# Longer weight runs through a permuted head layout, and a down projection that makes a row in four column tiles

## The chip, the cores and the metric

The kernel runs on one core of a Trainium2 chip. The metric is the device time of one execution in microseconds (us). Executions of the same kernel differ, so a difference of one microsecond needs several runs.

## The reference

One decoding step of one transformer block with adaptive layer norm: batch 1, width D = 640, 32 heads of 128, a cache of 16384 positions per head, a gated FFN of width F = 1728. The cut:

```
mod = silu(c) @ w_mod                       # six rows of 640: sa, ca, ga, sb, cb, gb
h = layernorm(x) * (1 + ca) + sa
for each of 32 heads: q = h @ wq ; scores = q . K / sqrt(128) ; o = softmax(scores) @ V
x = x + ga * (concat(o) @ wo)               # wo: 4096 x 640
h = layernorm(x) * (1 + cb) + sb
x = x + gb * ((silu(h @ w_gate) * (h @ w_up)) @ w_down)   # w_down: 1728 x 640
```

K and V are 32 x 2 loads of 4 MB each in bf16; everything else together is about 22 MB.

## The kernel before

Per head: VectorE multiplies the K tile by q (`mult`) and adds its halves (`fold1`); TensorE sums the rest with an identity (`fold`); VectorE finishes the scores (`red`, `max`); POOL takes the maximum over partitions (`gm`); ScalarE makes `exp`; TensorE makes P·V in four column tiles. A step called `diag` then transposes the result into a column, ScalarE scales it (`on`), and TensorE applies that head's output weights (`wo`). K and V have two buffers each. All large loads are issued in one fixed order by one queue (SP), and an issue that has to wait for a free buffer holds back all issues behind it.

The parts that matter (cuts marked ...; the numbers are positions in each engine's program):

```
# output weights: 4 heads a load, each row of wo a run of 640 * 2 = 1280 bytes
d_wo[g] = plan.dma(..., woring[:, g % 2], A_wo[g*G*128:(g+1)*G*128, :].rearrange("(g p) n -> p g n", p=128), ...)
# a V load may start only when P.V of two heads earlier is done
vdeps = [o_pvlast[h - 2]] if h >= 2 else [o_mod_a, o_mod_b]
...
# transposing step: 4 matmuls (fp32: 8 instructions) per head, then scale, then 5 output matmuls
def f_diag(e):
    for i in range(4):
        e.matmul(OT_ps[:, h:h+1], lhsT=acc_sb[:, s2, 128*i:128*(i+1)], rhs=sel[:, i:i+1], start=(i == 0), stop=(i == 3))
o_on[h] = op(ACT, vbase + 10.0, ... On[:, h:h+1] <- OT_ps[:, h:h+1] * rl[:, h:h+1])
o_wo[h] = op(PE, vbase + 10.5, ... 5 matmuls)
...
# down weights in three pieces: 1600 KB, 80 KB, 480 KB; a column of the output per 5 matmuls
NJA = FJ - 3
d_wd = [dma(wd_v[:, 0:NJA]), dma(wdr_v[0:FR]), dma(wd_v[:, NJA:FJ])]
for j in js:
    for cc in range(KC):
        e.matmul(f_ps[:, cc:cc+1], lhsT=wv[:, cc, :], rhs=gu_col[0:kw, j:j+1], ...)
# output: 128 runs of 10 bytes
d_out = plan.dma(..., out[0, 0].rearrange("(p k) -> p k", k=KC), o_col[:], ...)
```

## Time and profile before

693.03 us, median of three runs (691.93 to 693.73).

| | before |
|---|---|
| span of the profiled run | 690.0 us |
| read from HBM | 290.5 MB |
| DMA queue 1, share of 16 engines' span | 98.8% |
| DVE, PE, POOL, ACT busy | 66%, 44%, 41%, 12% |
| last weights landed (landing records) | 684.36 us |
| from there to the end | 5.65 us |

From the page of the kernel before, the slice line of the DMA engines, the packet line and two of the queues (queue: packets, MB, share):

```profile
DMA  9999999999999999999999999999999999999995
DMA packets 16398, 290.86 MB, mean 422 GB/s; under 512 B 1458, under 2 KB 7284, under 8 KB 7284
q1 hardware_dynamic: 16368, 290.48, 98.8%
q8 instruction: 20, 0.33, 0.2%
```

The engines are full from the second microsecond to the last slice: the kernel is bound by DMA. Of 16368 packets 5824 are the 1280-byte rows of output and down weights.

DMA is not busy without a break.

The packet records put the idle time of the average engine between 650 and 660 us at 0.78 us. Why, the chain of work that ended last tells (start us, us, what; these lines are not adjacent):

```profile
650.19 3.56 PE psb L436 x30
653.77 0.33 SPq L71
...
657.13 25.75 DMA kring<-in_B_w_down_dram
```

P·V of head 29 ends at 653.77 us, and at that moment SP issues the last V load, which needs that buffer. The loads queued before it run out at about the same time.

The tail, from the timeline of the kernel before (start us, us, engine, line, operation, tiles, count, [idle before it and what ended it]; the lines of LDWEIGHTS and one of DVE left out):

```profile
680.62 0.17 DVE L515 TENSOR_TENSOR gu_col<-psb,sg 128x14 bf16<-128x14 f32 x1 [2.78 <-PE psb L506]
683.02 3.37 PE L523 MATMUL psb<-gu_col,kring 128*128 128x1 bf16 x70 [2.51 <-DMA kring<-in_B_w_down_dram]
686.43 0.16 DVE L529 TENSOR_TENSOR tt<-psb,mod_col 128x5 f32<-128x5 f32 x1 [5.63 <-PE psb L523]
686.82 0.36 SPq L71 DMA_DIRECT2D out_dram<-o_col  x1
```

PE has its operand at 680.8 us and waits for the 1600 KB piece until 682.9; then all 70 matmuls still have to run.

Last, a late head (timeline of the kernel before; lines of LDWEIGHTS, DVE and POOL left out):

```profile
593.10 0.40 ACT L421 ACTIVATE P_sb<-S_sb,nb 128x128 bf16<-128x128 f32 x1
593.41 0.18 ACT L421 ACTIVATION_READ_ACCUMULATOR P_sb<-S_sb,nb 128x1 f32 x1
593.50 0.24 ACT L462 ACTIVATE On<-psb,rl 128x1 bf16<-128x1 f32 x1
593.64 0.39 ACT L385 ACTIVATE R_sb<-ident,q_r 128x128 bf16<-128x128 bf16 x1
...
593.80 0.36 PE L470 MATMUL psb<-On,woring 128*128 128x1 bf16 x5 [10.04 <-ACT On L462]
...
594.30 3.48 PE L436 MATMUL psb<-vring,P_sb 128*32 128x512 bf16 x32
```

Each ScalarE instruction starts about 0.1 us before the one ahead of it ends. From the end of the exp instruction (593.50) to P·V it is 0.80 us, and it is 0.80 to 0.81 us in each of the twelve heads whose P·V follows an exp directly rather than waiting for V (the first, the last ones and the one after the long wait for V at 527 us, which have less ahead of P·V, apart).

### The profile page before, as it was taken

What the parts mean: (1) busy time and instruction counts of PE and PEld (TensorE: products, weight loads), DVE (VectorE), ACT (ScalarE), POOL (GpSimd) and SP (SyncE); (2) the same over time, 40 slices, a digit from 0 to 9 for tenths busy, and PEclk for the clock granted to TensorE, in tenths of its full rate; (3) what the DMA queues carried; (4) which work ended last, traced back from release to release, by engine and by line L of the source; (5) the groups of instructions that cost most, each with busy time, mean ns of one, the idle gap of its engine ahead of it and who ended that gap; (6) DMA issues with size and microseconds to landing.
All of it is one profiled execution on the core that took longest, in us unless ns stands there. A gap on an engine that the chain in (4) does not pass through costs nothing.

```text
span 690.0 us, 5939 instructions
## 1 busy us (share of the span) xinstructions
PE 305.9 (44%) x2602; PEld 150.5 (22%) x2602; DVE 453.8 (66%) x151; ACT 80.1 (12%) x306; POOL 280.4 (41%) x75
## 2 busy tenths in 40 slices
PE   1503454545444334455432455444335345454464
PEld 1401122222212122222111222212112122221144
DVE  0077767676778876657787566668766676767800
ACT  0100101111111111110111111101011011111110
POOL 0006666565677554000405033304054365667700
PEclk9997666666767666666766666657666666767675
DMA  9999999999999999999999999999999999999995
GB/s 385 422 423 435 434 427 428 427 431 429 430 419 433 434 431 434 420 438 426 430 433 425 432 429 428 427 428 429 437 432 421 434 432 427 425 433 424 400 425 202
DMA packets 16398, 290.86 MB, mean 422 GB/s; under 512 B 1458, under 2 KB 7284, under 8 KB 7284
## 3 DMA queue, kind: packets, MB, share of 16 engines
q1 hardware_dynamic: 16368, 290.48, 98.8%
q8 instruction: 20, 0.33, 0.2%
q14 instruction: 6, 0.05, 0.0%
q10 hardware_dynamic: 4, 0.00, 0.0%
HBM read 290.47 MB, written 0.00 MB: 421 GB/s over the span
## 4 chain that ended last, share of the span: by engine, by line
DMA 40%; DVE 21%; PE 18%; POOL 18%; ACT 2%; issue 1%; SPq 1%
DMA kring<-in_A_k_cache_dram 36%; POOL gm L417 18%; DVE kring L397 13%; PE psb L407 9%; PE psb L436 7%; DVE f L399 6%; DMA kring<-in_B_w_down_dram 4%; DVE S_sb L411 2%; ACT P_sb L421 1%; PE psb L470 1%; DVE pm L414 1%; SPq L71 1%; PE psb L523 0%; PE psb L388 0%; ACT nb L419 0%
## 5 line engine op out<-in xcount | busy, mean ns | idle before, releaser
L397 DVE TENSOR_TENSOR kring<-kring,qbc_sb 128x16384 bf16<-128x16384 bf16 x32 | 278.0, 8687 | 30.2 <-DMA kring<-in_A_k_cache_dram 28.5
L417 POOL PARTITION_ALL_REDUCE gm<-pm x32 | 136.7, 4272 | 333.5 <-DVE pm L414 327.5
L436 PE MATMUL psb<-vring,P_sb 128*32 128x512 bf16 x992 | 108.6, 616 | 138.3 <-DMA vring<-in_A_v_cache_dram 138.3
L424 POOL PARTITION_ALL_REDUCE Ls<-rs x32 | 140.7, 4396 | 27.3 <-ACT P_sb L421 27.3
L407 PE MATMUL psb<-f,ident 128*128 128x512 bf16 x512 | 135.0, 421 | 27.9 <-DVE f L399 27.9
L399 DVE TENSOR_TENSOR f<-kring 128x8192 bf16<-128x8192 bf16 x32 | 141.6, 4425 | 1.1
L411 DVE TENSOR_REDUCE S_sb<-psb 128x128 f32<-128x512 f32 x32 | 22.1, 692 | 153.2 <-PE psb L407 153.2
L470 PE MATMUL psb<-On,woring 128*128 128x1 bf16 x160 | 11.6, 182 | 160.7 <-ACT On L462 159.7
L407 PEld LDWEIGHTS psb<-f,ident 128*128 128x128 bf16 x512 | 50.7, 104 | 120.5 <-DVE f L399 49.5
L436 PEld LDWEIGHTS psb<-vring,P_sb 128*32 128x32 bf16 x992 | 33.5, 138 | 190.8 <-DMA vring<-in_A_v_cache_dram 140.4
L470 PEld LDWEIGHTS psb<-On,woring 128*128 128x128 bf16 x160 | 8.9, 130 | 162.3 <-ACT On L462 162.3
L419 ACT ACTIVATE nb<-gm 128x1 f32<-128x1 f32 x32 | 6.5, 203 | 307.6 <-POOL gm L417 307.6
L447 PEld LDWEIGHTS psb<-sel,acc_sb 128*128 128x128 f32 x248 | 32.3, 191 | 5.8 <-ACT acc_sb L441 1.2
L441 ACT ACTIVATE acc_sb<-psb 128x512 f32<-128x512 f32 x31 | 18.5, 597 | 117.9 <-PE psb L436 117.8
L447 PE MATMUL psb<-sel,acc_sb 128*128 128x1 f32 x248 | 29.4, 240 | 0.7 <-ACT acc_sb L441 0.7
L426 ACT ACTIVATE lnl<-Ls 128x1 f32<-128x1 f32 x32 | 6.4, 201 | 115.8 <-POOL Ls L424 115.8
L388 PE MATMUL psb<-R_sb,ones_bf 128*128 128x128 bf16 x32 | 8.3, 259 | 23.6 <-ACT R_sb L385 23.6
L421 ACT ACTIVATE P_sb<-S_sb,nb 128x128 bf16<-128x128 f32 x32 | 12.8, 401 | 1.0
L385 ACT ACTIVATE R_sb<-ident,q_r 128x128 bf16<-128x128 bf16 x32 | 12.5, 389 | 0.0
L391 ACT ACTIVATE qbc_sb<-psb 128x128 bf16<-128x128 f32 x32 | 8.9, 277 | 11.2 <-PE psb L388 11.2
L414 DVE TENSOR_REDUCE pm<-S_sb 128x1 f32<-128x128 f32 x32 | 9.2, 286 | 1.1
L308 POOL PARTITION_ALL_REDUCE st<-st x2 | 0.8, 391 | 20.8 <-DVE x L488 11.2
(62 smaller groups left out, 80.3 us busy)
## 6 DMA issues: line engine op xcount, KB each, us to landing
kring<-in_A_k_cache_dram SPq DMA_DIRECT2D x32, 4096.0 KB, 25.6
vring<-in_A_v_cache_dram SPq DMA_DIRECT2D x31, 4096.0 KB, 34.4
wreg<-in_A_wq_dram SPq DMA_DIRECT2D x1, 5120.0 KB, 27.1
woring<-in_A_wo_dram SPq DMA_DIRECT2D x8, 640.0 KB, 25.5
vring<-in_w_mod_dram SPq DMA_DIRECT2D x1, 4800.0 KB, 14.3
vring<-in_A_v_cache_dram SPq DMA_DIRECT2D x4, 1024.0 KB, 9.7
wreg<-in_B_w_gate_dram SPq DMA_DIRECT2D x1, 2160.0 KB, 16.7
wreg<-in_B_w_up_dram SPq DMA_DIRECT2D x1, 2160.0 KB, 21.6
```

What stands on the lines that cost most here:

```text
L397: o_mult[h] = op(DVE, base, lambda e, kslot=kslot, qb=qb: e.tensor_tensor(out=kslot, in0=kslot, in1=qb, op=ALU.mult), deps=[d_k[h], o_qbc[ ...
L399: o_fold1[h] = op(DVE, base + 8.8, lambda e, kslot=kslot: e.tensor_tensor(out=f1[:], in0=kslot[:, :, 0:64], in1=kslot[:, :, 64:128], op=AL ...
L407: r = e.matmul(S_ps[s2][:].rearrange("p (t r) -> p t r", r=GC), lhsT=ident[:], rhs=f1[:, :, GC * m:GC * (m + 1)], start=(m == 0), stop=(m ...
L411: o_red[h] = op(DVE, base + 17.0, lambda e, s2=s2: e.tensor_reduce(out=S_sb[:, s2], in_=S_ps[s2][:].rearrange("p (t r) -> p t r", r=GC), a ...
L414: o_max[h] = op(DVE, base + 19.3, lambda e, h=h, s2=s2: e.tensor_reduce(out=pm[:, h:h + 1], in_=S_sb[:, s2], axis=AX.X, op=ALU.max), deps= ...
L417: o_gm[h] = op(POOL, base + 19.6, lambda e, h=h: e.partition_all_reduce(gm[:, h:h + 1], pm[:, h:h + 1], channels=128, reduce_op=bass.bass_ ...
L421: o_exp[h] = op(ACT, base + 20.4, lambda e, h=h, s2=s2, sp=sp: e.activation(out=P_sb[:, sp, 0:TT], in_=S_sb[:, s2], func=ACTF.Exp, scale=S ...
L424: o_L[h] = op(POOL, base + 21.0, lambda e, h=h: e.partition_all_reduce(Ls[:, h:h + 1], rs[:, h:h + 1], channels=128, reduce_op=bass.bass_i ...
L436: r = e.matmul(acc_ps[s2][q4:q4 + 32, :], lhsT=P_sb[:, sp, 4 * j:4 * j + 32], rhs=vring[:, s2, 4 * j:4 * j + 4, :].rearrange("p a d -> p ( ...
L441: o_acc[h] = op(ACT, vbase + 9.0, lambda e, s2=s2: e.activation(out=acc_sb[:, s2, :], in_=acc_ps[s2][:], func=ACTF.Copy), deps=[o_pvlast[h ...
L447: r = e.matmul(OT_ps[:, h:h + 1], lhsT=acc_sb[:, s2, 128 * i:128 * (i + 1)], rhs=sel[:, i:i + 1], start=(i == 0), stop=(i == 3))
L470: r = e.matmul(attn_ps[:, cc:cc + 1], lhsT=wv[:, cc, :], rhs=On[:, h:h + 1], start=(h == 0 and cc == 0), stop=(h == H - 1 and cc == KC - 1 ...
```

## The change

The intent has two parts. **Part 1**: for seven of the eight groups of four heads, load the output weights so that a partition gets four consecutive rows, a run of 5120 bytes. Partition p then holds rows 4p to 4p+3, so the attention output has to be laid out the same way: `diag` writes it in 32-row pieces (16 fp32 matmuls, 32 instructions per head), each head is scaled on its own 32 partitions, and the output matmuls of four heads come together. **Part 2**: the down weights come in five pieces, the last of 160 KB; the down projection makes a row (each column tile 160 wide) so that four matmuls per 128 rows run side by side; gate and residual are needed as rows too; the output goes out as four runs of 320 bytes. The buffers for P also fall from 6 to 4 (NP in the diff).

The diff, cut to its core:

```
-    NP = 6
+    NP = 4
+        o_gbrmm = op(PE, 1.2, f_gbr, ...)                       # gate row, 20 matmuls at the start
-                                   A_wo[...].rearrange("(g p) n -> p g n", p=128), ...
+                                   A_wo[...].rearrange("(g p) n -> p g n" if lastg else "(p g) n -> p g n", g=G), ...
-                    for i in range(4):
-                        r = e.matmul(OT_ps[:, h:h + 1], lhsT=acc_sb[:, s2, 128 * i:128 * (i + 1)], ...)
+                    for j in range(1 if lastg else G):
+                        for i in range(4):
+                            blk = acc_sb[:, s2, 128 * i:128 * (i + 1)]
+                            if lastg: dst = OT_ps[:, h:h + 1]
+                            else:
+                                dst = OT_ps[32 * hq:32 * hq + 32, h - hq + j:h - hq + j + 1]
+                                blk = blk.rearrange("p (m j) -> p j m", j=G)[:, j, :]
+                            r = e.matmul(dst, lhsT=blk, rhs=sel[:, i:i + 1], start=(i == 0), stop=(i == 3))
+                qs = slice(32 * hq, 32 * hq + 32)
+                on_dst, on_src, on_sc = On[qs, h - hq:h - hq + G], OT_ps[qs, h - hq:h - hq + G], rl[qs, h:h + 1]
-            o_wo[h] = op(PE, vbase + 10.5, f_wo, ...)           # 5 matmuls each head
+            elif hq == G - 1:
+                o_wo[h] = op(PE, vbase + 10.5, lambda e, h=h: f_wo(e, h + 1 - G, h + 1), ...)   # 20 every fourth
-        NJA = FJ - 3
+        wd_cut = [(0, 5), (5, 9), None, (9, FJ - 1), (FJ - 1, FJ)]
+        o_x1rmm = op(PE, TE + 0.25, f_x1r, ...)                 # x1 as a row, 20 fp32 matmuls
-                for cc in range(KC):
-                    r = e.matmul(f_ps[:, cc:cc + 1], lhsT=wv[:, cc, :], rhs=gu_col[0:kw, j:j + 1], ...)
+                for g in range(4):
+                    r = e.matmul(f_ps[32 * g:32 * g + 1, 0:RW], lhsT=gu_col[0:kw, j:j + 1], rhs=wv[:, RW * g:RW * (g + 1)], ...)
-        d_out = plan.dma(..., out[0, 0].rearrange("(p k) -> p k", k=KC), o_col[:], ...)
+        d_out = plan.dma(..., out[0, 0].rearrange("(g n) -> g n", g=4), o_row[0:128:32, :], ...)
```

More of the change, by code (lines that the diff above doesn't have):

```diff
@@ L164, in build @@
     GC = 4
+    RW = D // 4
     G = 4
-    NP = 6
+    NP = 4
     LASTP = 4
@@ L215, in build @@
         sel = sb("sel", [128, GC], F32)
-        cx_row = sb("cx_row", [1, 2, D], BF16)
+        identf = sb("identf", [128, 128], F32)
+        gb_row = sb("gb_row", [128, RW], F32)
+        x1_row = sb("x1_row", [128, RW], F32)
+        t3_row = sb("t3_row", [128, RW], F32)
+        o_row = sb("o_row", [128, RW], BF16)
+        cx_row = f1[0:1].rearrange("p t d -> p (t d)")[:, 0:2 * D].rearrange("p (v n) -> p v n", v=2)
         mod_col = sb("mod_col", [128, NMOD], F32)
@@ L238, in build @@
         gu_col = sb("gu_col", [128, FCH], BF16)
-        tt3 = sb("tt3", [128, KC], F32)
-        o_col = sb("o_col", [128, KC], BF16)
         psb = [es.enter_context(nc.psum_tensor("psb%d" % i, [128, 512], F32)) for i in range(8)]
@@ L253, in build @@
         f_ps = psb[0]
+        x1r_ps = psb[1]
+        gbr_ps = psb[3]
         acc_ps = [psb[6], psb[7]]
@@ L266, in build @@
             out=sel[:], in_=ident[:].rearrange("p (g r) -> p r g", g=4)[:, 0:GC, :], axis=AX.X, op=ALU.add), deps=[o_ident], name="sel")
+        o_idf = op(DVE, 0.12, lambda e: e.tensor_copy(out=identf[:], in_=ident[:]), deps=[o_ident], name="identf")
+        o_zgb = op(DVE, 0.01, lambda e: e.memset(gbr_ps[:, 0:RW], 0.0), name="zero_gbr")
         d_c = plan.dma(-1.0, cx_row[:, 0, :], c_in[0:1, :], "c", eng="act", name="dma_c")
@@ L301, in build, with f_gbr @@
         o_mod_b = op(PE, 1.1, lambda e: f_mod(e, modb_ps, NA, NMOD), deps=[d_wm, o_sc], name="mod_mm_b")
+        def f_gbr(e):
+            r = None
+            for k in range(KC):
+                for g in range(4):
+                    r = e.matmul(gbr_ps[32 * g:32 * g + 1, 0:RW], lhsT=silu_c[:, k:k + 1], rhs=wm_v[:, k, 5 * D + RW * g:5 * D + RW * (g + 1)],
+                                 start=(k == 0), stop=(k == KC - 1))
+            return r
+        o_gbrmm = op(PE, 1.2, f_gbr, deps=[d_wm, o_sc, o_zgb], name="gb_row_mm")
+        o_gbr = op(ACT, 1.96, lambda e: e.activation(out=gb_row[:], in_=gbr_ps[:, 0:RW], func=ACTF.Copy), deps=[o_gbrmm], name="gb_row")
         o_modc_a = op(ACT, 1.5, lambda e: e.activation(out=mod_col[:, 0:NA], in_=moda_ps[:, 0:NA], func=ACTF.Copy), deps=[o_mod_a], name="mod_col_a")
@@ L371, in build @@
             last = h == H - 1
+            lastg = h // G == H // G - 1
+            hq = h % G
             d_k[h] = plan.dma(qpos["k", h], kring[:, s2], kv(A_k, h), ("k", s2),
@@ L376, in build @@
                 d_wo[g] = plan.dma(qpos["wo", g], woring[:, g % 2],
-                                   A_wo[g * G * 128:(g + 1) * G * 128, :].rearrange("(g p) n -> p g n", p=128), ("wo", g % 2),
+                                   A_wo[g * G * 128:(g + 1) * G * 128, :].rearrange("(g p) n -> p g n" if lastg else "(p g) n -> p g n", g=G), ("wo", g % 2),
                                    deps=[o_wo[(g - 1) * G - 1]] if g >= 2 else [], name="dma_wo%d" % g)
@@ L380, in build @@
             VP = TT // nvp
-            vdeps = [o_pvlast[h - 2]] if h >= 2 else [o_mod_a, o_mod_b]
+            vdeps = [o_pvlast[h - 2]] if h >= 2 else [o_mod_a, o_mod_b, o_gbrmm]
             d_v[h] = [plan.dma(qpos["v", h] + 0.01 * c, vring[:, s2, c * VP:(c + 1) * VP, :], kv(A_v, h)[:, c * VP:(c + 1) * VP, :],
@@ L442, in build, with f_diag @@
                               deps=[o_pvlast[h], o_diag[h - 2] if h >= 2 else None], name="acc%d" % h)
-                def f_diag(e, h=h, s2=s2):
+                def f_diag(e, h=h, s2=s2, hq=hq, lastg=lastg):
                     r = None
-                    for i in range(4):
-                        r = e.matmul(OT_ps[:, h:h + 1], lhsT=acc_sb[:, s2, 128 * i:128 * (i + 1)], rhs=sel[:, i:i + 1],
-                                     start=(i == 0), stop=(i == 3))
+                    for j in range(1 if lastg else G):
+                        for i in range(4):
+                            blk = acc_sb[:, s2, 128 * i:128 * (i + 1)]
+                            if lastg:
+                                dst = OT_ps[:, h:h + 1]
+                            else:
+                                dst = OT_ps[32 * hq:32 * hq + 32, h - hq + j:h - hq + j + 1]
+                                blk = blk.rearrange("p (m j) -> p j m", j=G)[:, j, :]
+                            r = e.matmul(dst, lhsT=blk, rhs=sel[:, i:i + 1], start=(i == 0), stop=(i == 3))
                     return r
@@ L461, in build, with f_wo @@
                 o_pvlast[h] = o_diag[h] = prev
-            o_on[h] = op(ACT, vbase + 10.0, lambda e, h=h: e.activation(
-                out=On[:, h:h + 1], in_=OT_ps[:, h:h + 1], func=ACTF.Copy, scale=rl[:, h:h + 1]),
-                deps=[o_diag[h], o_rl[h]], name="on%d" % h)
-            def f_wo(e, h=h):
-                r = None
-                wv = woring[:, (h // G) % 2, h % G, :].rearrange("p (m j) -> p j m", j=KC)
-                for cc in range(KC):
-                    r = e.matmul(attn_ps[:, cc:cc + 1], lhsT=wv[:, cc, :], rhs=On[:, h:h + 1],
-                                 start=(h == 0 and cc == 0), stop=(h == H - 1 and cc == KC - 1), skip_group_check=True)
-                return r
-            o_wo[h] = op(PE, vbase + 10.5, f_wo, deps=[o_on[h], d_wo[h // G]], name="wo%d" % h)
+            if lastg:
+                on_dst, on_src, on_sc = On[:, h:h + 1], OT_ps[:, h:h + 1], rl[:, h:h + 1]
+            else:
+                qs = slice(32 * hq, 32 * hq + 32)
+                on_dst, on_src, on_sc = On[qs, h - hq:h - hq + G], OT_ps[qs, h - hq:h - hq + G], rl[qs, h:h + 1]
+            o_on[h] = op(ACT, vbase + 10.0, lambda e, a=on_dst, b=on_src, c=on_sc: e.activation(out=a, in_=b, func=ACTF.Copy, scale=c),
+                         deps=[o_diag[h], o_rl[h]], name="on%d" % h)
+            def f_wo(e, c0, c1):
+                r = None
+                for c in range(c0, c1):
+                    wv = woring[:, (c // G) % 2, c % G, :].rearrange("p (m j) -> p j m", j=KC)
+                    for cc in range(KC):
+                        r = e.matmul(attn_ps[:, cc:cc + 1], lhsT=wv[:, cc, :], rhs=On[:, c:c + 1],
+                                     start=(c == 0 and cc == 0), stop=(c == H - 1 and cc == KC - 1), skip_group_check=True)
+                return r
+            if lastg:
+                o_wo[h] = op(PE, vbase + 10.5, lambda e, h=h: f_wo(e, h, h + 1), deps=[o_on[h], d_wo[h // G], o_gbr], name="wo%d" % h)
+            elif hq == G - 1:
+                o_wo[h] = op(PE, vbase + 10.5, lambda e, h=h: f_wo(e, h + 1 - G, h + 1), deps=[o_on[h], d_wo[h // G], o_gbr], name="wo%d" % h)
         TE = T0 + (H - 1) * PERIOD + 10.5 + PERIOD * lead(H - 1) + 20.0
@@ L479, in build @@
         wd_src = B_wd[0:128 * FJ, :].rearrange("(j p) n -> p j n", p=128)
-        NJA = FJ - 3
-        d_wd = [plan.dma(QE + 0.02, wd_v[:, 0:NJA], wd_src[:, 0:NJA], "wd0", deps=[o_fold1[H - 2]], name="dma_wd0"),
-                plan.dma(QE + 0.03, wdr_v[0:FR], B_wd[128 * FJ:F, :], "wdr", deps=[o_fold1[H - 2]], name="dma_wdr"),
-                plan.dma(QE + 0.04, wd_v[:, NJA:FJ], wd_src[:, NJA:FJ], "wd1", deps=[o_fold1[H - 2]], name="dma_wd1")]
+        wd_cut = [(0, 5), (5, 9), None, (9, FJ - 1), (FJ - 1, FJ)]
+        d_wd = []
+        for n, c in enumerate(wd_cut):
+            if c is None:
+                d_wd.append(plan.dma(QE + 0.02 + 0.01 * n, wdr_v[0:FR], B_wd[128 * FJ:F, :], ("wd", n), deps=[o_fold1[H - 2]], name="dma_wd%d" % n))
+            else:
+                d_wd.append(plan.dma(QE + 0.02 + 0.01 * n, wd_v[:, c[0]:c[1]], wd_src[:, c[0]:c[1]], ("wd", n), deps=[o_fold1[H - 2]], name="dma_wd%d" % n))
         o_abf = op(ACT, TE, lambda e: e.activation(out=attn_bf[:], in_=attn_ps[:, 0:KC], func=ACTF.Copy), deps=[o_wo[H - 1]], name="attn_bf")
@@ L515, in build, with f_x1r @@
         o_gum = op(DVE, TE + 1.7, lambda e: e.tensor_tensor(out=gu_col[:], in0=u_ps[:, 0:FCH], in1=sg[:], op=ALU.mult), deps=[o_sg, o_u], name="gu")
+        o_zx = op(DVE, TE - 0.8, lambda e: e.memset(x1r_ps[:, 0:RW], 0.0), deps=[o_qbc[H - 1], o_qbc[H - 2]], name="zero_x1r")
+        o_zf = op(DVE, TE - 0.7, lambda e: e.memset(f_ps[:, 0:RW], 0.0), deps=[o_qbc[H - 1], o_qbc[H - 2]], name="zero_f")
+        def f_x1r(e):
+            r = None
+            for k in range(KC):
+                for g in range(4):
+                    dst = x1r_ps[32 * g:32 * g + 1, 0:RW].rearrange("o (m j) -> o j m", j=KC)[:, k, :]
+                    r = e.matmul(dst, lhsT=x1[:, k:k + 1], rhs=identf[:, 32 * g:32 * (g + 1)],
+                                 start=(k == 0), stop=True, skip_group_check=True)
+            return r
+        o_x1rmm = op(PE, TE + 0.25, f_x1r, deps=[o_x1, o_zx, o_idf], name="x1_row_mm")
+        o_x1r = op(ACT, TE + 1.25, lambda e: e.activation(out=x1_row[:], in_=x1r_ps[:, 0:RW], func=ACTF.Copy), deps=[o_x1rmm], name="x1_row")
         def f_down(e, js, first, fin):
@@ L520, in f_down @@
                 kw = 128 if j < FJ else FR
-                wv = (wd_v[:, j, :] if j < FJ else wdr_v[0:FR, :]).rearrange("p (m i) -> p i m", i=KC)
-                for cc in range(KC):
-                    r = e.matmul(f_ps[:, cc:cc + 1], lhsT=wv[:, cc, :], rhs=gu_col[0:kw, j:j + 1],
-                                 start=(first and j == js[0] and cc == 0), stop=(fin and j == js[-1] and cc == KC - 1), skip_group_check=True)
-            return r
-        o_dn = op(PE, TE + 1.8, lambda e: f_down(e, list(range(NJA)), True, False), deps=[o_gum, d_wd[0], o_qbc[H - 2], o_qbc[H - 1]], name="down_a")
@@ L527, in build @@
-        o_dn = op(PE, TE + 1.82, lambda e: f_down(e, [FJ], False, False), deps=[o_dn, d_wd[1]], name="down_r")
-        o_dn = op(PE, TE + 1.85, lambda e: f_down(e, list(range(NJA, FJ)), False, True), deps=[o_dn, d_wd[2]], name="down_b")
-        o_t3 = op(DVE, TE + 1.9, lambda e: e.tensor_tensor(out=tt3[:], in0=f_ps[:, 0:KC], in1=mod_col[:, 5 * KC:6 * KC], op=ALU.mult),
-                  deps=[o_dn], name="gb_ffn")
-        o_oc = op(DVE, TE + 2.0, lambda e: e.tensor_tensor(out=o_col[:], in0=tt3[:], in1=x1[:], op=ALU.add), deps=[o_t3], name="o_col")
@@ L532, in build @@
-        d_out = plan.dma(QE + 2.0, out[0, 0].rearrange("(p k) -> p k", k=KC), o_col[:], "out", deps=[o_oc], name="dma_out")
+                wv = wd_v[:, j, :] if j < FJ else wdr_v[0:FR, :]
+                for g in range(4):
+                    r = e.matmul(f_ps[32 * g:32 * g + 1, 0:RW], lhsT=gu_col[0:kw, j:j + 1], rhs=wv[:, RW * g:RW * (g + 1)],
+                                 start=(first and j == js[0]), stop=(fin and j == js[-1]), skip_group_check=True)
+            return r
+        o_dn = None
@@ new lines, in build @@
+        for n, c in enumerate(wd_cut):
+            js = [FJ] if c is None else list(range(*c))
+            o_dn = op(PE, TE + 1.8 + 0.01 * n, lambda e, n=n, js=js: f_down(e, js, n == 0, n == len(wd_cut) - 1),
+                      deps=[o_gum, d_wd[n], o_zf, o_dn], name="down%d" % n)
+        o_t3 = op(DVE, TE + 1.9, lambda e: e.tensor_tensor(out=t3_row[:], in0=f_ps[:, 0:RW], in1=gb_row[:], op=ALU.mult),
+                  deps=[o_dn, o_gbr], name="gb_ffn")
+        o_oc = op(DVE, TE + 2.0, lambda e: e.tensor_tensor(out=o_row[:], in0=t3_row[:], in1=x1_row[:], op=ALU.add), deps=[o_t3, o_x1r], name="o_row")
@@ L533, in build @@
+        d_out = plan.dma(QE + 2.0, out[0, 0].rearrange("(g n) -> g n", g=4), o_row[0:128:32, :], "out", deps=[o_oc], name="dma_out")
         plan.op("sp", QE + 3.0, lambda e: e.nop(), deps=[d_out], name="final_wait")
```

## The prediction

> **What bounds the kernel now.** The DMA engines. The page gives 290.9 MB in a 690.0 us span, and DMA reads 9 in every slice but the last; queue 1 takes 98.8% of 16 engines' span. The packet records of the trace show idle time only at the start (2.0 us before the engines fill), a hole of about 0.8 us near 653-658 us (the last V load waits for P·V of head 29, which ends at 653.8 us) and the tail. DVE is busy 66%, PE 44%. So DMA time removed is time saved, and so is time after the last landing.
>
> **Part 1, output weights.** In the packet records 1280-byte packets of this load take 58.3 ns (22 B/ns), 32 KB packets 1219 ns (26.9 B/ns), 8 KB packets about 309 ns (26.5 B/ns). One group of 512 small packets is 1.87 us of 16 engines; the small packets overlap a little (records sum to 1.05 of the engines), so its real cost is about 1.75 us; the issue times of successive K loads stretch by 1.7 to 1.8 us in two of the three places with such a load in the DMA-paced middle. The same bytes in 128 packets of 5 KB (estimate 195 ns each, from the 8 KB rate) cost 1.56 us. Seven of eight groups change: 7 x 0.2 to 0.3 = 1.4 to 2.1 us. I take 1.5 us.
>
> Cost on PE: the transposing step after P·V goes from 8 to 32 instructions per head, perhaps +1 us, but after it PE waits some 10 us for the POOL maximum: free. Output-projection matmuls come 20 every fourth head instead of 5 each (0.36 us per five): neutral.
>
> **Part 2, tail.** The last weights land at 684.36 us. PE starts the down projection only when the 1600 KB piece lands (682.89 us), runs 70 matmuls in 3.4 us, ends at 686.4; output issued 686.82, landed 689.6. After: five pieces, so all but the last four matmuls are done when the last 160 KB land. The Trainium skill, "TensorE: Matmul & The Clock Gate", Part 3, says column tiles run concurrently; this trace agrees (P·V's 32 four-tile N=512 matmuls take 3.4 us, 106 ns each, against up to 421 ns for whole-array ones). So 14 x about 0.15 us of row matmuls keep up with the DMA, and PE ends about 0.5 us after the last landing: 1.5 us saved. DVE on 160 columns costs about 0.3 us more. The output as four runs instead of 128 of 10 bytes saves perhaps 0.4 us of the 2.8; the rest is fixed: "DMA: Bandwidth & Descriptors", anatomy of one DMA, puts most of the fixed cost in the write receipt. Net 1.6 us.
>
> **Added elsewhere.** Gate row by 20 matmuls at the start (about 1 us before the first V issue, with 30 us of loads queued: free). x1 row by fp32 matmuls between x1 and gate (about 2 us in a 2.6 us window, and up waits for its weights until 678.2 us anyway): free.
>
> **Predicted:** 693.0 - 1.5 - 1.6 = 689.9 us, range 688.2 to 691.5. Faster by over 2%: 0.01; within 2%: 0.98; slower: 0.01.
>
> **Right if** the profile shows 3584 small packets gone, 896 of 5 KB near 195 ns, the last weights landing 1 to 2 us earlier, and landing-to-end falling from 5.6 to about 4 us. **Wrong if** the hole before the last V load grows by what DMA saves (the compute chain of the last heads is nearly as long as the DMA's period), if column-tiled single-row matmuls do not overlap (7.5 us, past the last landing), or if the longer transposing step delays the chain of POOL, P·V and fold.

## More of the kernel before

All runs here were of the state "fast" (one core, no second state seen).

From the windows of the kernel before (window: us, then busy us and count of PE, PEld, DVE, ACT, POOL, then the granted clock, the DMA share, GB/s):

```profile
650.00:660.00 10.00, 9.00 (x61) 3.94 (x59) 4.17 (x5) 1.18 (x5) 3.71 (x2) 0.72 0.87 355
```

The share is 0.87 where it is 1.00 to 1.01 in the other ten-microsecond windows between the start and the tail.

## The result, and the profile after

690.75 us, median of four runs (690.33 to 691.77); before, 692.99 us (691.93 to 693.73, four runs). The ratio is 0.9971, 95% interval 0.9954 to 0.9988. Ratios in this document are the mean time of one kernel's fast runs over that of the other's of the same rounds, so not quite the ratio of the medians quoted. A second measurement (experiment e9) gave 0.9972.

From the page of the changed kernel:

```profile
DMA packets 13613, 290.96 MB, mean 422 GB/s; under 512 B 1354, under 2 KB 3596, under 8 KB 4492
q1 hardware_dynamic: 13576, 290.48, 98.7%
q8 instruction: 26, 0.43, 0.2%
```

The small packets are gone: in the packet records 896 packets of 5120 bytes take 198.5 ns each, against 58.3 ns for each of the 3584 that they replace. The starts of the output-weight loads in the DMA-paced middle (some 220 to 540 us, where the chain waits for its K load at nearly every head) come every 79.28 us instead of 79.49: 0.21 us saved per group, as estimated. The load just ahead of the last V load lands at 656.11 us instead of 657.82. So DMA is 1.7 us ahead there by its slowest engine, 1.0 by the mean of the sixteen. But now the windows and the chain of the changed kernel:

```profile
650.00:660.00 10.00, 8.19 (x61) 3.86 (x61) 5.76 (x7) 1.76 (x7) 4.12 (x3) 0.75 0.68 268
```

```profile
651.67 3.52 PE psb L458 x32
655.20 0.33 SPq L71
...
676.70 8.35 DMA kring<-in_B_w_down_dram
```

P·V of head 29 ends at 655.20 us instead of 653.77, and the last V load is issued that much later. The DMA share there fell from 0.87 to 0.68; the idle time of the average engine grew from 0.78 to 2.88 us. All that part 1 had saved went into waiting for this one issue, and more: the last weights land at 685.45 us, 1.1 us later than before. The tail, from the timeline of the changed kernel (lines of LDWEIGHTS left out):

```profile
681.76 0.17 DVE L556 TENSOR_TENSOR gu_col<-psb,sg 128x14 bf16<-128x14 f32 x1 [3.21 <-PE psb L547]
...
685.82 0.30 PE L578 MATMUL psb<-kring,gu_col 128*1 128x160 bf16 x4 [0.16 <-PE psb L578]
686.18 0.32 DVE L586 TENSOR_TENSOR t_row<-psb,gb_row 128x160 f32<-128x160 f32 x1 [4.24 <-PE psb L578]
686.53 0.33 DVE L588 TENSOR_TENSOR o_row<-t_row,x_row 128x160 bf16<-128x160 f32 x1
686.88 0.63 SPq L71 DMA_DIRECT2D out_dram<-o_row  x1
```

From the last landing to the end it is now 3.46 us instead of 5.65: part 2 gains 2.2 us. PE ends 0.70 us after the last landing instead of 2.0; the two VectorE steps cost 0.3 us more; from issue to the output's landing it is 1.64 us (686.88 to 688.52) instead of 2.79.

Why is P·V of head 29 later? The stretch from exp to P·V of the same head as above, from the timeline of the changed kernel:

```profile
592.54 0.40 ACT L443 ACTIVATE P_sb<-S_sb,nb 128x128 bf16<-128x128 f32 x1
592.85 0.19 ACT L443 ACTIVATION_READ_ACCUMULATOR P_sb<-S_sb,nb 128x1 f32 x1
593.06 0.26 ACT L497 ACTIVATE On<-psb,rl 32x4 bf16<-32x4 f32 x1
593.35 0.40 ACT L407 ACTIVATE R_sb<-ident,q_r 128x128 bf16<-128x128 bf16 x1
...
594.02 3.33 PE L458 MATMUL psb<-vring,P_sb 128*32 128x512 bf16 x32
```

The scale instruction `On` no longer starts before its predecessor ends but 0.02 us after it, and neither does the next one: two overlaps of 0.1 us have become two gaps. The pattern holds in all heads where P·V follows an exp directly. For the first head of each group of four, whose 32 partitions start at partition 0, exp to P·V stays at 0.80 us; for the second and third (partitions 32 and 64) it is 1.07; for the fourth (partition 96), where the 20 output matmuls (0.96 us) also stand ahead of P·V, it is 1.45:

```profile
630.47 0.40 ACT L443 ACTIVATE P_sb<-S_sb,nb 128x128 bf16<-128x128 f32 x1
...
631.30 0.96 PE L505 MATMUL psb<-On,woring 128*128 128x1 bf16 x20 [8.95 <-ACT On L497]
...
632.32 3.60 PE L458 MATMUL psb<-vring,P_sb 128*32 128x512 bf16 x32
```

The scale instruction has the same shape (32x4) in all these heads, so its starting partition is what differs. Over the five heads that lead to the last V load this adds 1.17 us. The rest of the 1.7 us by which this chain grew is in the fold's 16 matmuls, which take 3.6 to 6.6 us with the phase of the TensorE clock: 25.3 us in these six folds before, 25.8 after. That part differs from run to run, as the experiments show.

### The profile page after: what moved, and what is told of

Same layout as the page of the kernel before. It is cut to its first block, busy times and chain, and to the rows that moved or that the text cites. A ratio compares the mean times of both kernels' runs of the same rounds, so it can differ in the third digit from the quotient of the medians.

```text
span 688.9 us, 7385 instructions
## 1 busy us (share of the span) xinstructions
PE 336.4 (49%) x3320; PEld 173.8 (25%) x3320; DVE 454.4 (66%) x155; ACT 85.3 (12%) x308; POOL 292.9 (43%) x75
## 4 chain that ended last, share of the span: by engine, by line
DMA 37%; DVE 21%; POOL 18%; PE 17%; SPq 3%; ACT 2%; issue 1%
DMA kring<-in_A_k_cache_dram 36%; POOL gm L439 18%; DVE kring L419 13%; PE psb L429 9%; PE psb L458 7%; DVE f L421 6%; SPq L71 3%; DVE S_sb L433 2%; DMA kring<-in_B_w_down_dram 1%; ACT P_sb L443 1%; DVE pm L436 1%; ACT R_sb L407 1%; PE psb L410 0%; ACT nb L441 0%; ACT On L497 0%
## 5 line engine op out<-in xcount | busy, mean ns | idle before, releaser
L439 POOL PARTITION_ALL_REDUCE gm<-pm x32 | 145.1, 4534 | 319.2 <-DVE pm L436 314.2
L446 POOL PARTITION_ALL_REDUCE Ls<-rs x32 | 145.0, 4532 | 27.4 <-ACT P_sb L443 27.4
L429 PE MATMUL psb<-f,ident 128*128 128x512 bf16 x512 | 132.1, 414 | 27.8 <-DVE f L421 27.5
L478 PEld LDWEIGHTS psb<-sel,acc_sb 128*32 128x32 f32 (+1 forms) x920 | 58.9, 157 | 13.8 <-issue 11.9
L478 PE MATMUL psb<-sel,acc_sb 128*32 128x1 f32 (+1 forms) x920 | 61.2, 200 | 0.7 <-ACT acc_sb L463 0.7
L410 PEld LDWEIGHTS psb<-R_sb,ones_bf 128*128 128x128 bf16 x32 | 3.3, 104 | 129.5 <-ACT R_sb L407 129.5
L505 PE MATMUL psb<-On,woring 128*128 128x1 bf16 x160 | 8.1, 180 | 41.7 <-ACT On L497 41.7
L505 PEld LDWEIGHTS psb<-On,woring 128*128 128x128 bf16 x160 | 7.3, 131 | 42.6 <-ACT On L497 42.6
```

The source lines that it names most:

```text
L429: r = e.matmul(S_ps[s2][:].rearrange("p (t r) -> p t r", r=GC), lhsT=ident[:], rhs=f1[:, :, GC * m:GC * (m + 1)], start=(m == 0), stop=(m ...
L439: o_gm[h] = op(POOL, base + 19.6, lambda e, h=h: e.partition_all_reduce(gm[:, h:h + 1], pm[:, h:h + 1], channels=128, reduce_op=bass.bass_ ...
L446: o_L[h] = op(POOL, base + 21.0, lambda e, h=h: e.partition_all_reduce(Ls[:, h:h + 1], rs[:, h:h + 1], channels=128, reduce_op=bass.bass_i ...
L478: r = e.matmul(dst, lhsT=blk, rhs=sel[:, i:i + 1], start=(i == 0), stop=(i == 3))
```

## The experiments

The theory: part 1 saves about 1.4 us of DMA, but the hole before the last V load gives it back, since the compute chain of the last heads grew; part 2 is worth about 2 us. The rivals: the larger hole is chance; the 5 KB runs save nothing; the five pieces disturb the queue. Twelve runs, each five rounds (e2 and e9 left six times), all correct; e1 to e4 share one chip, e5 to e8 another, e9 to e12 a third:

| run | median us | before, same chip | ratio (95%) |
|---|---|---|---|
| e1 part 1 alone | 692.48 | 691.71 | 1.0006 (0.9994 to 1.0018) |
| e2 part 2 alone | 691.19 | 691.71 | 0.9982 (0.9968 to 0.9997) |
| e3 hole filled with down weights | 691.29 | 691.71 | 0.9993 (0.9980 to 1.0006) |
| e4 P·V ahead of all else | 694.77 | 691.71 | 1.0034 (1.0022 to 1.0046) |
| e5 hole filled with up weights | 689.89 | 691.79 | 0.9971 (0.9957 to 0.9984) |
| e6 the same with old output weights | 689.46 | 691.79 | 0.9961 (0.9949 to 0.9974) |
| e7 five pieces alone, old column form | 690.52 | 691.79 | 0.9983 (0.9970 to 0.9997) |
| e8 chain put back | 689.17 | 691.79 | 0.9958 (0.9945 to 0.9970) |
| e9 the changed kernel again | 690.69 | 692.48 | 0.9972 (0.9960 to 0.9985) |
| e10 chain put back and hole filled | 689.25 | 692.48 | 0.9952 (0.9940 to 0.9965) |
| e11 e6 with more instructions | 690.66 | 692.48 | 0.9971 (0.9959 to 0.9983) |
| e12 e6 again | 689.27 | 692.48 | 0.9954 (0.9942 to 0.9967) |

### e1: part 1 alone

The edit: the kernel before with the output-weight, `diag`, `on` and `wo` lines of the diff, and nothing else of it.

> Kernel before plus the output-weight layout alone (5 KB runs, 32 transposing instructions, attention output scaled in 32-partition pieces, 20 output matmuls every fourth head); old tail. Theory (what the DMA saves is given back in the hole before the last V load, because the compute chain of the last heads got about 1.2 us longer): within 0.7 us of the kernel before; idle DMA time of 650 to 660 us between 2 and 3.5 us instead of 0.8; the steps from exp to P.V read 0.80, 1.07, 1.07, 1.45 us by head in the group. Rival (the larger hole is chance, the phase of the TensorE clock): 1.2 to 1.6 us faster than before, hole near 1 us. Rival (the 5 KB runs save nothing): the load before the hole lands no earlier than 657.8 us.

Measured: 0.8 us slower by the medians, ratio 1.0006, so no gain. Idle time 650 to 660 us: 2.2 us (DMA share 0.74). The load ahead of the hole landed at 656.24 us, 1.6 us earlier than before, so the runs do save. Exp to P·V: 0.80, 1.07, 1.07, 1.45. The theory's numbers hold. The rival that the runs save nothing falls; the rival "chance" had foreseen 1.2 to 1.6 us less time and misses it, but see e2.

### e2: part 2 alone

The edit: the changed kernel with those same lines put back.

> Changed kernel with the old output-weight layout: the new tail alone. Theory: the tail's gain is kept whole, 2.0 to 2.4 us faster than before, as fast as the whole change; hole near 0.8 us, exp to P.V 0.80 us in every head, last landing to end 3.4 to 3.6 us. Rival (both parts add up): about 1 us or more slower than the whole change, that is 0.8 to 1.2 us faster than before. Rival (five weight pieces delay the queue): the last weights land over 0.5 us later than 684.4 us.

Measured: last landing to end 3.50 us, exp to P·V 0.80 us, as expected. The time was only 0.5 us below before by the medians (1.2 by the means). The expected 2.0 to 2.4 us were missed, and so was the expected hole of 0.8 us: it was 2.0 us in its profile, with exp to P·V unchanged. The gain lies where the rival "both parts add up" had it (0.8 to 1.2 us), but e1 shows no gain for the other part to add. In the profile the fold of the head that leaves the DMA-paced stretch ran 6.59 us, against 5.25 before, nearly all of it at the slow TensorE clock (mean granted clock 0.54 over this fold, against 0.69 before and 1.00 in a fold of 3.6 us). The profiled run (692.05 us) was the slowest of the six; two were 689.4. So the hole has a part of about a microsecond that differs from run to run, and the rival "chance" is right for that part. It can't explain e1 or the pattern by heads. This also means that a single profile's hole is no measure of a change; the stretch from exp to P·V is.

### e3: fill the hole with down weights

```
-  d_wd.append(plan.dma(QE + 0.02 + 0.01 * n, wd_v[:, c[0]:c[1]], ...))
+  d_wd.append(plan.dma(qpos["v", H - 1] - 0.5 + 0.01 * n if n < 2 else QE + 0.02 + 0.01 * n, wd_v[:, c[0]:c[1]], ...))
```

> Changed kernel, but the first two pieces of the down-projection weights (1440 KB) are issued ahead of the last V load, so the DMA engines have work while that load waits for P.V of head 29. Theory (DMA is idle 2.9 us there and everything after is shifted by it): idle time of 650 to 660 us under 0.5 us, last landing 2 to 3 us earlier, time 1.5 to 2.2 us below the changed kernel (the up projection's wait for its weights limits the rest), about 4 us below before. Rival (the hole is not on the path to the end): same time as the changed kernel.

Measured: the hole is gone (DMA share 0.98) and the last landing is 1.5 us earlier, at 683.94 us, yet the kernel is no faster than before. The timeline of e3 (lines left out) says why:

```profile
682.25 2.25 PE L547 MATMUL psb<-h_col,wreg 128*128 128x1 bf16 x70 [4.22 <-DMA wreg<-in_B_w_up_dram]
684.61 0.17 DVE L556 TENSOR_TENSOR gu_col<-psb,sg 128x14 bf16<-128x14 f32 x1 [5.67 <-PE psb L547]
684.83 0.84 PE L578 MATMUL psb<-kring,gu_col 128*1 128x160 bf16 x20 [0.33 <-DVE gu_col L556]
...
688.96 0.64 SPq L71 DMA_DIRECT2D out_dram<-o_row  x1
```

The up weights now land almost last (682.2 us instead of 679.4), and they have the up projection, the gate product and the whole down projection behind them. What fills a hole has to be taken from what is needed late without much after it, and the order of the rest counts. The theory's expected gain was wrong, its hole was right.

### e4: P·V ahead of all else

```
# shortened
-  o_qbcmm[h] = op(PE, base - 14.8 if h > 0 ...)          +  base - 6.4      # after the fold
-  o_qbc[h]   = op(ACT, base - 14.6 if h > 0 ...)         +  base - 0.45
-  o_wo[h] = op(PE, vbase + 10.5, ...)                    +  vbase + 23.2    # after the fold; heads 30, 31 as they were
```

> Changed kernel, with the output-projection matmuls and the q broadcast placed after the fold instead of ahead of P.V on PE, so P.V waits for exp alone. Theory (the chain exp, attention scale, q row, 20 matmuls, P.V delays the last V issue): exp to P.V under 0.4 us in every head of the last ones, the last V load issued 2.5 to 4 us earlier, hole under 1 us, time 1.5 to 3 us below the changed kernel. Rival (the longer transposing step or the fold's clock phase made the hole): hole stays over 2 us and the time is within 0.5 us of the changed kernel.

Measured: the hole is gone and the last weights land at 682.84 us, 2.6 us earlier than in the changed kernel, but the kernel is 3 us slower than before: from the last landing to the end it is 10.6 us. The measure "exp to P·V" lost its meaning here, because P·V needs only an earlier head's exp; the matmuls ahead of it had been what tied it to the moment. Freed of them, it ran right after `diag`, ten microseconds ahead of the fold. From the timeline of e4, a fold, a P·V and the next fold:

```profile
601.06 6.29 PE L429 MATMUL psb<-f,ident 128*128 128x512 bf16 x16 [10.35 <-DVE f L421]
...
609.27 1.90 PE L458 MATMUL psb<-vring,P_sb 128*32 128x512 bf16 x29
...
621.51 6.30 PE L429 MATMUL psb<-f,ident 128*128 128x512 bf16 x16 [10.34 <-DVE f L421]
```

A fast fold, from the timeline of the kernel before:

```profile
635.37 3.63 PE L407 MATMUL psb<-f,ident 128*128 128x512 bf16 x16
```

PE idled 10.35 us ahead of the fold, and the fold ran 6.29 us instead of 3.6 to 4.7. The Trainium skill, "TensorE: Matmul & The Clock Gate", Part 1, says that the array's clock is halved after an idle window of some 3.4 us and restored after as long a busy one; this run agrees: the mean granted clock is 0.57 over this fold, 1.00 over a fast one, and most of its weight loads start 0.43 us apart, in a fast fold 0.2. The slow part lasts some 5 us here, longer than one such window. The old order, as far as these lines tell, let P·V (3.5 us) warm the clock for the fold, which is on the way to the next head's scores. Every late head got some 1.3 us longer (20.4 us from one `mult` to the next, against 19.2 in the changed kernel), and the end became compute-bound. So the work ahead of P·V was not simply a delay; its timing was worth keeping.

### e5 and e6: fill the hole with up weights, with new and old output weights

```
+  d_wu0 = plan.dma(qpos["v", H - 1] - 0.5, wu_v[:, 0:3], wu_src[:, 0:3], "wu0", deps=[o_qmm], ...)
-  d_wu  = plan.dma(QE + 0.01, wu_v, ...)
+  d_wu  = plan.dma(QE + 0.01, wu_v[:, 3:KC], wu_src[:, 3:KC], "wu", deps=[o_qmm], ...)
```

e6 is the same edit on e2, the kernel with the old output weights.

> Changed kernel, with the first three fifths of the up-projection weights (1296 KB, about 3 us of DMA) issued ahead of the last V load instead of down-projection pieces; the remaining order is V, gate, rest of up, down. The earlier fill failed because the up weights then landed last (682.2 us) with 8 us of dependent work behind them; here they land at about 676 us. Theory (idle DMA time before the last V load is on the path when what lands last has little work behind it): idle time of 650 to 660 us under 0.5 us, last landing at 682.5 to 683.5 us, end 2 to 3 us below the changed kernel, 4 to 5 us below before. Rival (compute from the last V load to the end is the limit anyway): within 0.7 us of the changed kernel.

> The same fill with the old output-weight layout (1280-byte runs), all else as in the run before this one. Theory (the 5 KB runs do save 1.4 us of DMA, but only a filled hole lets it reach the end): 1.0 to 1.7 us slower than the run with the fill and the 5 KB runs. Rival (the output-weight layout saves nothing at all): equal within 0.4 us.

Measured: e5 lies 1.9 us below before by the medians, e6 2.3 us. Their profiles end 0.9 and 1.2 us earlier than the changed kernel's, not 2 to 3. The main expectation failed: with the hole nearly closed (0.5 us in e5, none in e6), the 5 KB runs bring no gain at all. The landings show how it went. The output-weight saving was there at the end of V, where the median engine of e5 was 0.95 us ahead of e6 (667.93 and 668.88 us); at the last weights it was 0.25 ahead, and the slowest engine was behind (684.53 against 684.12 us). Something ate it between, engine by engine. e8, e11 and e12 follow that up.

### e7: five pieces alone

The edit: the kernel before with the `wd_cut` lines of the diff and the old column-form matmuls, each piece's waiting for its own load.

> Kernel before, with the down-projection weights in the five pieces of the change and the old column form (70 matmuls, output of 10-byte runs). Theory (most of the tail's gain is that matmuls no longer all wait for the 1600 KB piece): last landing to end falls from 5.65 us to 4.1 to 4.6 us, so 1.1 to 1.5 us of the 2.2 us; the rest, 0.7 to 1.1 us, is the row form and its four output runs. Rival (the row form is what gains): landing to end over 5.2 us.

Measured: last landing to end 4.43 us, inside the expected range; ratio 0.9983. In this profile (the slowest of the five runs) the last weights landed at 686.24 us, 1.9 us later than before, which looks like the rival "the five pieces disturb the queue"; e2's landed 1.4 us later too. But the mean landing of the last weights follows the mean landing of the last V piece by 16.8 us in all of before, e1 (three pieces), after, e2 and e7 (five pieces), 16.84, 16.79, 16.85, 16.85 and 16.78, so the pieces cost nothing: what differs stood before the last V load, or is one slow engine (in e7 2.8 us behind the mean). So 1.2 us of the tail's 2.2 come from not waiting for one 1600 KB piece, and 0.9 from the row form and its output. Issue to output landing is 2.6 us here and 1.64 in the row form, which alone accounts for the 0.9.

### e8: the chain put back

```
# shortened
-  out=rl[:, h:h + 1], in_=lnl[:, h:h + 1]
+  out=rl[32*(h%G):32*(h%G)+32, h-h%G:h-h%G+1], in_=lnl[32*(h%G):32*(h%G)+32, h:h+1]    # heads below H - G
-  on_dst, on_src, on_sc = On[qs, h-hq:h-hq+G], OT_ps[qs, ...], rl[qs, h:h+1]             # each head
+  on_dst, on_src, on_sc = On[:, h-hq:h-hq+G], OT_ps[:, ...], rl[:, h-hq:h-hq+1]          # every fourth head
-  o_wo[h] = op(PE, vbase + 10.5, ...20 matmuls)
+  o_wo[h] = op(PE, vbase + 23.2, ...20 matmuls)
```

> Changed kernel, but the attention output of four heads is scaled by one ScalarE instruction over all 128 partitions at the fourth head (the reciprocals are written per 32 partitions off the chain instead), and the 20 output matmuls come after the fold; the q broadcast stays ahead of P.V. Theory (ScalarE instructions that start at partition 32, 64 or 96 do not overlap their neighbours and lengthen exp to P.V by 0.27 us, the 20 matmuls by 0.37 us more): exp to P.V 0.65 to 0.85 us in every head, the last V load issued 0.8 to 1.6 us earlier than in the changed kernel, up to the phase of the TensorE clock; time 0.3 to 1.3 us below the changed kernel. Rival: no difference in exp to P.V, or a difference there that does not move the V load.

Measured, from the timeline of e8:

```profile
610.61 0.40 ACT L443 ACTIVATE P_sb<-S_sb,nb 128x128 bf16<-128x128 f32 x1
610.91 0.19 ACT L443 ACTIVATION_READ_ACCUMULATOR P_sb<-S_sb,nb 128x1 f32 x1
611.00 0.39 ACT L407 ACTIVATE R_sb<-ident,q_r 128x128 bf16<-128x128 bf16 x1
...
611.67 2.75 PE L460 MATMUL psb<-vring,P_sb 128*32 128x512 bf16 x24
```

Exp to P·V is 0.66 us where no scale instruction stands, 0.81 where one does. The last V load is issued at 652.61 us, 2.6 us earlier than in the changed kernel and more than expected: over the five heads exp to P·V adds up to 3.38 us instead of 4.98, and the six folds happened to be 0.6 us shorter. The hole is about 0.9 us, the last weights land at 683.61, and the median is 2.6 us below before (the changed kernel in e9: 1.8 below). The intervals of e8 and e9 overlap, so the gain of about 0.8 us over the changed kernel is told by the trace rather than by the times. That part 1 with its chain put back keeps part of what it saves is suggested (the last weights land 0.9 us earlier than before by the mean of the engines, in one profile each) and not shown: no run sets e8 beside e2 on one chip.

### e9, e10, e11, e12: the changed kernel, a combination, and the price of instructions

e9 is the changed kernel unedited. e10 is e8 with the fill of e5, two fifths of the up weights instead of three. e12 is e6 again. e11 is e12 with

```
-  for i in range(4):
+  for i in (list(range(4)) * G if h < H - G else range(4)):     # diag repeated four times, same result
```

> The changed kernel itself, unedited, timed on the same chip as the three that follow. All theories: 1.2 to 2.6 us faster than before; the hole before the last V load between 2 and 3 us; 26 instruction fetches of 16 KB in the trace against 20 before.

> Candidate for a version that beats both: the chain put back as in the earlier run (one scale instruction per four heads, the 20 output matmuls after the fold), and two fifths of the up weights (864 KB) ahead of the last V load to fill what is left of the hole (0.96 us there). Theory: idle DMA time of 650 to 660 us under 0.3 us, last landing near 682.7 us, time 0.5 to 1.2 us below the run with the chain put back alone (which was 0.42% below before), so 3.2 to 4 us below before. Rival (lagging DMA engines decide the last landing): no better than 0.5% below before, with the mean landing of the last weights nevertheless 0.7 us earlier than 682.0 us.

> Filled kernel with the OLD output-weight layout, with the old transposing step repeated four times for the first 28 heads (same result, 32 instead of 8 instructions per head, as many as the 5 KB layout needs). Theory (each 16 KB instruction fetch takes one DMA engine 1.06 us, and the 5 KB layout's additional PE instructions cost six of them): 25 or 26 fetches instead of 20, mean landing of the last weights 0.3 to 0.5 us later than in the filled kernel with the old layout, time 0.2 to 1.0 us slower. Rival (instruction fetches are free): equal within 0.2 us, same mean landing.

> The filled kernel with the old output-weight layout once more, unedited, so that the run before this one has its partner on the same chip. 20 fetches; 0.3 to 0.5% below before; mean landing of the last weights near 682.1 us.

Measured: e9 repeats the result, with a hole of 3.9 us in its profile (its slowest run), more than the 2 to 3 expected. e12 is as expected. e11 is 1.4 us slower than e12 (690.21 to 690.77 against 689.18 to 689.75: no overlap), more than the theory's 0.2 to 1.0, although its chain is the same (exp to P·V 0.80 us), its bytes are the same and neither has a hole. From the pages of e12, then e11:

```profile
q8 instruction: 20, 0.33, 0.2%
```

```profile
q8 instruction: 26, 0.43, 0.3%
```

With the additional matmul instructions there are six more fetches of 16 KB. In the packet records each such fetch is one packet of about 1.06 us (mean 1047 ns in e12, 1065 in e11); six are 0.4 us of 16 engines, and the mean landing of the last weights is 0.56 us later in e11 (682.52 against 681.96). The rest is unevenness: a load lands in sixteen parts, one for each engine, and a part that has fallen behind stays behind in the loads after it. The trace doesn't name the engines; that the laggard is the one that fetched is inferred from the times. In the kernel before, no engine is more than 0.5 us behind the median when the load of 636 us lands; a fetch starts at 638.8 us, and one engine is 2.0 us behind from the next landing on; after a fetch at 668.8 us there are two, after one at 676.5 three. The kernel waits for the slowest. In e11 the last engine is 3.05 us behind the mean, in e12 1.97. But the unevenness does not follow the number of fetches: the last engine is 2.83 us behind the mean in e7, with 20, and 1.61 in e8, with 26. That more instructions cost 1.4 us in this kernel is measured; that they cost it through these fetches is inferred from times that fit, and was not isolated, and 1.4 us is no price that carries over to another kernel.

The 5 KB layout needs the same additional instructions (32 instead of 8 per head in 28 heads) and has the same 26 fetches. With e11's 1.4 us as their price in a filled kernel and e5 only 0.4 us slower than e6, the 5 KB runs themselves save about 1.0 us by subtraction across two chips (a rough estimate; the DMA-paced middle shows 7 x 0.21 = 1.5 us). Why e5 is no faster than e6 therefore stays open in part.

e10 is the lowest by ratio (0.9952) but no better than e12 (0.9954): its hole is 0.5 us (under 0.3 expected), its mean landing 682.00 us, not 0.7 earlier as both the theory and the rival had it, and its last engine is 2.10 us behind. Both e10 and e12 beat both kernels: every run of theirs lies at 689.75 us or below, every run of the changed kernel beside them at 690.11 or above. e12, which has part 2 and the fill and leaves out part 1, is the simpler one.

## Why the prediction was right or wrong

- **Bound by DMA, with a small hole before the last V load: right.** The hole was seen and named as a danger; then it was not costed. The prediction's own "Wrong if the hole before the last V load grows by what DMA saves" came true: 0.78 to 2.88 us in the profiles, against 1.5 saved.
- **Part 1, 1.5 us of DMA: right in size, wrong in where it went.** Packets at 198.5 ns (195 predicted), 0.21 us a group (0.2 to 0.3), 1.7 us earlier at the hole. But in e1 the time did not fall at all.
- **The step that failed: "DMA time removed is time saved", with "Cost on PE: free" and "neutral".** The scale instructions on partitions 32, 64 and 96 added 0.27 us to exp to P·V, and 20 matmuls together added 0.37 us in front of one P·V; over the five heads that decide when the last V load can be issued this is 1.17 us, in the one place where the compute chain is the limit. "Free" also left out the instruction fetches: six more, where as many additional instructions cost 1.4 us in e11.
- **The term mis-sized the other way: the tail.** 1.6 us predicted, 2.2 measured in the traces. PE ended 0.70 us after the last landing (0.5 predicted), VectorE cost 0.3 us more (0.3), and the output's landing fell by 1.15 us instead of 0.4. The prediction leaned on the Trainium skill's page "DMA: Bandwidth & Descriptors" (anatomy of one DMA), which puts most of the fixed cost in the write receipt, and took the receipt for unchangeable. That passage is told for DMA issued by gpsimd (POOL), and this output is issued by SP; here 128 runs of 10 bytes took 2.79 us and four of 320 took 1.64. What in them costs the difference was not tested.
- **Last weights 1 to 2 us earlier: wrong**; they came 1.1 us later in the profile after and 2.5 us later in e9.
- **Column tiles overlap: right.** 20 single-row matmuls take 0.84 us, 42 ns each; the prediction's case without overlap, 7.5 us for 56, is 134 ns each. (Its 421 ns for a whole-array matmul is the mean length of one; from start to start it is 0.43 us at the slow clock, so the comparison stands.)
- **Added elsewhere, free: right.** The first V load is issued 1.0 us later (22.38 against 21.37 us), the 40 instructions of the x1 row take 0.71 us, and from x1 to the operand of the gate matmuls it is 2.56 us in both kernels.
- **The total: 689.9 predicted, 690.75 measured, inside the range.** Of 3.1 us predicted 2.2 came, because the larger gain of the tail covered the missing gain of part 1: two errors of opposite sign. That the total fell inside the range is in part luck. What each part is worth in time can be told only to about a microsecond, since the hole differs from run to run with the clock's phase.

## What to carry to other kernels

When a kernel is bound by one resource, look for the places where that resource waits for another chain: a saving upstream of such a place is lost there if the chain gets even slightly longer. Before filling a hole, ask what will then land last and how much work hangs on it; before moving work out of the way of a matmul, ask whether it kept TensorE at its fast clock. Count instructions too: here their fetches, six more of 16 KB, went over the same DMA engines.

## What the Trainium skill lacked or had wrong

- "DMA: Bandwidth & Descriptors", Specifications, gives 512 bytes as the least transfer for line rate. Here 1280-byte packets moved 22 B/ns per engine (58.3 ns), 5120-byte ones 25.8 (198.5 ns), 32 KB ones 26.9 (1219 ns); packets overlap a little, so the gap in time is smaller (0.21 us a group saved, where these times give 0.28).
- The same page tells "Anatomy of one DMA" for the gpsimd path only; no passage that I found gives the time of a small store issued by SP by its number of runs. Here the 1280 bytes of output took 2.79 us from issue to landing in 128 runs and 1.64 in four.
- No page that I found prices instruction fetches. Here each is one packet of 16 KB and 1.06 us, 20 to 26 in a run; in e11 additional instructions with six more fetches cost 1.4 us.
- No page that I found says that a ScalarE instruction on partitions from 32, 64 or 96 does not overlap its neighbours. Here, in all 21 such instructions of the changed kernel, it started 0.02 us after its predecessor's end instead of 0.09 us before, and so did the one after it; 0.27 us in all per such instruction.
